# Tau-masked attention with a gated FFN on one core: the last half block as a plain transpose, k and q loaded first, new planner numbers

## The chip, the cores and the metric

The kernel runs on one core of a Trainium2 chip. The metric is the device time of one execution in microseconds, the median of several runs; lower is better.

## What is computed

All tensors are float32 in memory, with batch 8, 8 heads, sequence 576, head width 64, and a hidden width of 1024.

```python
scores = scale * q @ k.T                       # per batch and head, 576 x 576
thresh = scores.max(-1) - tau
scores = where(scores >= thresh, scores, -1e9)
attn   = softmax(scores)                       # divided by sum + 1e-9
x      = (attn @ v), heads side by side        # 8 x 576 x 512
h      = relu(x @ w_in)                        # 512 -> 1024
gate   = sigmoid(conv3(h) along the sequence, one filter of 3 per channel)
out    = (h * gate) @ w_out                    # 1024 -> 512
```

## The kernel before

**Work.** A batch's 576 tokens are cut into tiles of 128 rows: four whole ones and one of 64. Tiles 0 and 1 make one chunk, tiles 2, 3 and 4 another, so there are 16 chunks, and for each chunk four pairs of heads: 64 pairs. A *unit* is one tile of one pair. For a whole tile it takes the two heads one after the other; for the tile of 64 rows both heads share the 128 partitions. Per unit:

- `mm` in `unit` (L442 for the first batch and for the 64-row tiles, on half arrays; L449 else) multiplies q and k into a PSUM buffer `ps_s`, of which there are two.
- `top` (L457, VectorE) takes the row maximum, `exp` (L463, ScalarE) the exponential into `em`, `limit` (L460) the threshold, `mask` (L466, VectorE) zeroes what is under it and sums. After the mask the `ps_s` buffer is free.
- `guard` (L483), a reciprocal (L490) and `even` (L487) give scale and shift, and `norm` (L495) normalises `em`.
- `transposes` turns `em` in blocks of 128 columns on TensorE (L519) into one of two PSUM buffers `ps_t`, and ScalarE copies them out to `eT` (L514). 576 columns are four and a half blocks. For whole tiles the two heads lie side by side, nine blocks; the ninth blocks of all tiles of a pair are collected in one `ps_t` buffer, `group(8, ...)`. In the 64-row tile the last half block of each head goes into the same buffer by `halves` (L534): two ordinary matmuls with half an identity, which put the heads' results on the lower and the upper 64 partitions.
- `attend` (L571) multiplies `eT` with v once per pair, and the result is split in a high and a low part `x`.

After the four pairs of a chunk, `mm1` (L600) computes a 128-channel slice of the hidden layer in three products of high and low parts, followed by ReLU, the three taps (L618, L627), a tanh and the gate. `mm2` (L665) multiplies the gated hidden values with `w_out`, again in three products, for 128 tokens at a time.

**Weights.** They arrive as 64-bit words and `split` turns each into a high and a low float32 part with two operations on ScalarE, two or three on VectorE and one or two on GpSimd. This happens in 16 pieces beside the attention of the first batch. The first three pieces are loaded by ScalarE's queue, all other loads by SyncE's.

**Order.** No order is written by hand. Every operation is entered by `op` with an engine, a cost in ns, a rank (the unit it belongs to, less an `ahead`), and sometimes other engines that may take it. `Plan.run` then plays the program: each engine takes the ready operation of lowest rank, operations may go to another engine when their own has more than `BACKLOG` ns in hand, `LATENCY` is the time from one engine's end to another's start, `SWITCH` the cost of a change of kind on TensorE ("rows" for L442, "cols" for L571, "turn" for L519 and L534, "full" for the rest), and `KEEP` how far in rank TensorE may look to avoid one. `WRATE` sets when weights are due, `MOE` how first-layer and second-layer pieces alternate. The order in which operations were taken is the order of each engine's instructions; on the chip an engine runs them strictly in that order, so a waiting instruction holds all behind it.

Of the kernel before, what the change touches and what calls it, by code (L numbers as in the profile page):

```python
# [20 lines left out]
AHEAD = {'s': 6.0, 't': 3.5, 'a': 3.5, 'prep': 4.0, 'w': 2.0, 'load': 4.25}  # L21

LATENCY = {"pe": 197.0, "act": 145.0, "dve": 130.0, "pool": 115.0, "sp": 2000.0}
HPB = 3
MOE = (2, 1)
BACKLOG = {'pool': 28000.0, 'dve': 500.0, 'act': 9000000000.0}
WRATE = (0.891, 1.015)
# [9 lines left out]
    "rows": {"cols": 190, "turn": 240, "full": 290}, "cols": {"rows": 230, "turn": 260, "full": 310},  # L37
    "turn": {"rows": 95, "cols": 95, "full": 85}, "full": {"rows": 95, "cols": 95, "turn": 5},
}

KEEP = 1.2
# [20 lines left out]
class Plan:  # L62
# [13 lines left out]
    def op(self, engine, ns, fn, w=(), r=(), ahead=0.0, other=None, kind=None):  # L76
# [15 lines left out]
        self.ops.append((((engine, ns), *(other or ())), self.rank - ahead, fn if other is not None else lambda e: fn(), before, bufs, kind))  # L92

    def run(self):
# [28 lines left out]
        while events:  # L123
            t = events[0][0]
            while events and events[0][0] <= t:
# [9 lines left out]
                elif kind == "done":  # L135
                    engine = taken[x]
                    for j in after[x]:
                        waits[j] -= 1
                        for e in came[j]:
                            late = 0.0 if e == engine == "pe" else LATENCY[engine] + (30.0 if e == "pool" != engine else 0.0)  # L140
# [66 lines left out]
def tile_tau_attention_gated_ffn(  # L207
# [54 lines left out]
    op("sp", 100, lambda: nc.sync.dma_start(tau_sb[:], tau.broadcast_to([P, 1])), w=[(tau_sb, 0)], ahead=100.0)  # L262
# [19 lines left out]

    def act(n, psum=False):
        return n * 0.833 + (170 if psum else 200)

    def dve(n, fixed=140):
        return n * 1.1 + fixed

    def pool(n):
        return n * 2.1 + 240  # L290

    def pool1(n):
        return n * 1.69 + 80

    def split(src, n, name, high, low, hr, lr, queue="sp"):
# [37 lines left out]
        op(queue, 450, load, w=[hi, lo], ahead=w + (AHEAD["load"] if queue == "sp" else 90))  # L333
        op("act", act(n), f0, w=[a], r=[hi], ahead=w)
        op("pool", n * 1.69 + 80, f1, w=[a], ahead=w, other=[("dve", 150 + n * 0.65)])
        op("dve", 150 + n * 0.55, f2, w=[a], ahead=w)
        op("dve", 150 + n * 1.1, f3, w=[a], r=[hi], ahead=w)
        op("dve", 150 + n * 1.1, f4, w=[a], r=[lo], ahead=w)
# [43 lines left out]
    def prep_rows(i, b, p, o, w, tag):  # L382
# [4 lines left out]
        op("sp", 450, lambda: nc.sync.dma_start(k[:], kp[b, p]), w=[(k, 0)], ahead=a + 2)  # L387
        op("sp", 450, lambda: nc.sync.dma_start(q[:], qd[b, p, :, :, o:o + w]), w=[(q, 0)], ahead=a + 2)
        op("act", act(2 * w), lambda: nc.scalar.activation(q[:], q[:], AF.Copy, scale=0.125), w=[(q, 0)], ahead=a)
        return k, q  # L390

    def prep_k(b, p, j, ks):
# [3 lines left out]
        op("sp", 820, lambda: nc.sync.dma_start(xk[:, :S], kd[b, p, :, j]), w=[(xk, 0)], ahead=a + 2)  # L396
# [7 lines left out]
    def prep_q(i, b, p, j, q1, q2):  # L404
# [4 lines left out]
        op("sp", 455, lambda: nc.sync.dma_start(xq[:], qd[b, p, :, j, o:o + w]), w=[(xq, 0)], ahead=a + 2)  # L409
# [6 lines left out]
    def load_v(i, b, p):  # L416
        vt = plan.buf(wk, "v", 2, [P, NBLK + 1, D], F32, f"v_{i}")
        op("sp", 820, lambda: nc.sync.dma_start(vt[:], vc[b, p]), w=[(vt, 0)], ahead=AHEAD["prep"])
        return vt

    def unit(u, k, q1, q2, o, n):
# [9 lines left out]
        tiny = [("pool", 290)]  # L431
        for h, js in enumerate(heads):
# [26 lines left out]
            def limit(e, nm=nm, th=th):  # L459
                engines[e].tensor_scalar(few[:rows, th], few[:rows, nm], -1.0, tau_sb[:rows], op0=ALU.mult, op1=ALU.subtract)  # L460
# [4 lines left out]
            def mask(ps=ps, th=th, view=view, total=total):  # L465
# [6 lines left out]
                "pe", 480 if q2 is None else 532, mm, w=[(ps, 0)],  # L472
                r=[(k, 0), (q1, 0)] if q2 is None else [(x, h) for x in (k, q1, q2)], ahead=a, kind="rows" if q2 is None else "full"
# [342 lines left out]
```

## Time and profile before

| | us |
|---|---|
| median of 3 runs (975.6 to 979.25) | 976.28 |
| the profiled execution's own time | 977.8 |
| its span, first to last instruction | 976.0 |
| TensorE busy | 925.7 |
| VectorE busy | 804.6 |
| GpSimd busy | 728.6 |
| ScalarE busy | 694.8 |

In the profile PE is TensorE's matmul, PEld its weight load, DVE is VectorE, ACT ScalarE, POOL GpSimd, SP SyncE; SPq and ACTq are the queues on which those engines issue DMAs. Rows name a source line, the tile written and the tiles read. In a timeline a row is start, duration, engine, line, operation, and, in brackets, how long the engine stood idle before it and what released it.

### The profile page before, as it was taken

To read this page: it belongs to the slowest core of one execution; us is meant where nothing else is said; L and a number is where in the kernel's file an instruction comes from. 1 tells how busy PE (TensorE), PEld (TensorE's weight loads), DVE (VectorE), ACT (ScalarE), POOL (GpSimd) and SP (SyncE) were. 2 spreads that over 40 slices of the span, in tenths; PEclk is the share of its full clock that TensorE was granted. 3 is DMA by queue.
4 is the path that set the end of the run, shared out by engine and by line. 5 is a ranking of instruction groups with operands and counts; after the bars stand their busy time and mean duration, and the time that the engine had idled before them with its cause. 6 is when DMAs were issued, how large, how long until landed. Compare 5 with 4: busy or idle time off the path is not lost.

```text
span 976.0 us, 19384 instructions
## 1 busy us (share of the span) xinstructions
PE 925.7 (95%) x6368; PEld 740.6 (76%) x6368; DVE 804.6 (82%) x1926; ACT 694.8 (71%) x1508; POOL 728.6 (75%) x1175
## 2 busy tenths in 40 slices
PE   3887779999999999999999999999999999999998
PEld 2554558878888878878888788887888878887796
DVE  4889989997988887887897879897897879988443
ACT  4766778777876778767876678777876778776443
POOL 3769898876888678887886769886776877786333
PEclk9999989999999999999999999999999999999999
DMA  6344223233322133213332223223332133311000
GB/s 224 122 146 142 80 85 115 73 91 98 94 93 80 61 104 112 85 53 105 99 106 63 81 84 108 86 74 95 104 99 76 52 102 109 100 50 46 23 22 33
DMA packets 56259, 87.26 MB, mean 89 GB/s; under 512 B 13152, under 2 KB 29536, under 8 KB 56160
## 3 DMA queue, kind: packets, MB, share of 16 engines
q1 hardware_dynamic: 55728, 84.46, 28.5%
q10 hardware_dynamic: 432, 1.57, 0.5%
q8 instruction: 51, 0.84, 0.4%
q14 instruction: 48, 0.39, 0.1%
HBM read 76.57 MB, written 9.44 MB: 88 GB/s over the span
## 4 chain that ended last, share of the span: by engine, by line
PE 74%; DVE 10%; POOL 7%; issue 3%; DMA 2%; ACT 2%; SPq 0%; POOLq 0%; DVEq 0%; ACTq 0%
PE ph L600 17%; PE po L665 17%; PE pa L571 13%; PE ps_t L519 12%; PE ps_s L449 11%; PE ps_s L442 3%; DVE em L466 3%; POOL em L495 3%; DMA q<-in_qd_dram 2%; DVE few L457 2%; POOL gl L280 2%; DVE t L627 1%; DVE t L634 1%; POOL t L618 1%; PE ps_t L534 1%
## 5 line engine op out<-in xcount | busy, mean ns | idle before, releaser
L495 POOL TENSOR_SCALAR em<-em,few 128x576 f32<-128x576 f32 x288 | 263.5, 922 | 42.4 <-DVE few L490 29.3
L466 DVE SCALAR_TENSOR_TENSOR em<-ps_s,few,em 128x576 f32<-128x576 f32 x288 | 230.1, 811 | 36.3 <-ACT em L463 30.2
L457 DVE TENSOR_REDUCE few<-ps_s 128x1 f32<-128x576 f32 x288 | 212.9, 750 | 56.1 <-PE ps_s L449 39.4
L600 PE MATMUL ph<-x,w1h 128*128 128x322 f32 (+1 forms) x1024 | 251.8, 309 | 0.9 <-ACT hp L615 0.6
L463 ACT ACTIVATE em<-ps_s,few 128x576 f32<-128x576 f32 x288 | 209.0, 740 | 42.0 <-DVE few L457 31.5
L514 ACT ACTIVATE eT<-ps_t 128x512 f32<-128x512 f32 (+2 forms) x384 | 193.8, 532 | 48.0 <-PE ps_t L519 44.8
L519 PE MATMUL ps_t<-ident,em 128*128 128x128 f32 x1280 | 191.5, 279 | 12.0 <-POOL em L495 8.1
L627 DVE SCALAR_TENSOR_TENSOR t<-hp,cw,t 128x255 f32<-128x255 f32 (+1 forms) x256 | 176.6, 693 | 29.8 <-POOL t L618 28.1
L519 PEld LDWEIGHTS ps_t<-ident,em 128*128 128x128 f32 x1280 | 148.9, 142 | 52.3 <-POOL em L495 17.4
L600 PEld LDWEIGHTS ph<-x,w1h 128*128 128x128 f32 x1024 | 177.5, 190 | 7.9 <-issue 3.9
L571 PE MATMUL pa<-eT,v 128*64 128x256 f32 (+1 forms) x1280 | 171.5, 415 | 0.0
L449 PE MATMUL ps_s<-ks,q 128*128 128x288 f32 x896 | 159.4, 306 | 7.8 <-DVE em L466 3.2
L600 PE MATMUL ph<-x,w1l 128*128 128x322 f32 (+1 forms) x512 | 152.1, 297 | 0.0
L449 PEld LDWEIGHTS ps_s<-ks,q 128*128 128x128 f32 x896 | 131.2, 189 | 23.3 <-issue 7.4
L571 PEld LDWEIGHTS pa<-eT,v 128*64 128x64 f32 x1280 | 87.1, 138 | 67.3 <-issue 7.5
L280 POOL TENSOR_TENSOR gl<-t,gh 128x321 fp32r<-128x321 f32 (+13 forms) x184 | 119.3, 660 | 12.2 <-ACT gh L644 10.6
L665 PE MATMUL po<-w2h,gh 128*128 128x512 f32 x288 | 118.4, 411 | 0.0
L665 PE MATMUL po<-w2h,gl 128*128 128x512 f32 x288 | 113.7, 395 | 2.2 <-POOL gl L280 2.2
L665 PE MATMUL po<-w2l,gh 128*128 128x512 f32 x288 | 113.3, 393 | 0.0
L618 POOL TENSOR_SCALAR t<-hp,cw 128x321 f32<-128x321 f32 (+1 forms) x128 | 71.9, 562 | 38.2 <-ACT hp L615 31.3
L600 PEld LDWEIGHTS ph<-x,w1l 128*128 128x128 f32 x512 | 97.3, 190 | 0.3
L280 POOL TENSOR_TENSOR ks<-xk,ks 64x576 fp32r<-64x576 f32 x56 | 81.7, 1460 | 16.5 <-ACT ks L398 10.2
(56 smaller groups left out, 1127.6 us busy)
## 6 DMA issues: line engine op xcount, KB each, us to landing
v<-in_vc_dram SPq DMA_DIRECT2D x64, 320.0 KB, 3.0
xk<-in_kd_dram SPq DMA_DIRECT2D x56, 288.0 KB, 2.9
xq<-in_qd_dram SPq DMA_DIRECT2D x112, 128.0 KB, 2.3
k<-in_kp_dram SPq DMA_DIRECT2D x36, 320.0 KB, 3.1
out_dram<-ot SPq DMA_DIRECT2D x36, 256.0 KB, 2.0
stage<-in_w_out_dram SPq DMA_DIRECT2D x8, 512.0 KB, 3.4
stage<-in_w_in_dram SPq DMA_DIRECT2D x5, 512.0 KB, 4.1
q<-in_qd_dram SPq DMA_DIRECT2D x28, 64.0 KB, 3.2
```

The lines of the kernel that those rows point to most:

```text
L280: engines[e].tensor_tensor(dst, x, y, op=ALU.subtract)
L449: nc.tensor.matmul(ps[:, c, :CH], lhsT=q[:, h, o:o + n], rhs=k[:, h, c * CH:(c + 1) * CH], start=(i == 0), stop=(i == 1))
L457: nc.vector.tensor_reduce(few[:rows, nm], ps[:rows, :, :CH], op=ALU.max, axis=mybir.AxisListType.XY, negate=True)
L463: nc.scalar.activation(view(), ps[:rows, :, :CH], AF.Exp, bias=few[:rows, nm])
L466: nc.vector.scalar_tensor_tensor(view(), ps[:rows, :, :CH], few[:rows, th], view(), op0=ALU.is_ge, op1=ALU.mult, accum_out=few[:rows, total])
L495: engines[e].tensor_scalar(sl, sl, few[:rows, 6 + h:7 + h], few[:rows, 8 + h:9 + h], op0=ALU.mult, op1=ALU.add)
L514: "act", act(w, True), lambda dst=dst, src=src: nc.scalar.activation(dst(), src(pt), AF.Copy),
L519: nc.tensor.transpose(out=pt[:, at:at + P], in_=em[:, b * P:(b + 1) * P], identity=ident[:])
L571: nc.tensor.matmul(pa[j * D:(j + 1) * D, :w], lhsT=vt[:, blk + j, :], rhs=eT[:, blk, :w], start=(r == 0), stop=(r == 4))
L600: nc.tensor.matmul(ph[:, :an], lhsT=w1[w][:, cb, fs], rhs=xs[cb][:, h, :an], start=(cb == 0 and i == 0), stop=(cb == NCB - 1 and i == 2))
L627: nc.vector.scalar_tensor_tensor(t[:, :kn], hp[:, k:kn + k], cw[:, 3 * f + k:3 * f + k + 1], t[:, :kn], op0=ALU.mult, op1=ALU.add)
L665: nc.tensor.matmul(po[:], lhsT=x[:, f, at:at + P], rhs=w[:, f, :], start=(f == 0 and i == 0), stop=(f == NFB - 1 and i == 2))
```

## The change

The change has four parts.

1. `halves` is gone. The 64-row tile's columns 448 to 575 are turned as an ordinary block of 128 (`turn` with block number 3.5). Its upper 64 partitions hold the wanted half block of both heads, and two copies of 64x64, instead of one of 128x64, carry them to `eT`, one of them to the other half of the partitions.
2. In `prep_rows` the first k is issued on ScalarE's queue ahead of the weights, the first q at the head of SyncE's. Where q is scaled for a whole tile, that is done in two halves, one for each head.
3. `limit` adds a stored `ntau` = -tau instead of subtracting tau, so that ScalarE can compute it too, and ScalarE is named among the engines for `limit` and `norm`.
4. The numbers of the planner change throughout, and with them the order of every engine. Some of the diff:

```diff
-AHEAD = {'s': 6.0, 't': 3.5, 'a': 3.5, 'prep': 4.0, 'w': 2.0, 'load': 4.25}
+AHEAD = {'s': 6.0, 't': 3.25, 'a': 3.5, 'prep': 4.0, 'w': 2.0, 'load': 4.0}
-LATENCY = {"pe": 197.0, "act": 145.0, "dve": 130.0, "pool": 115.0, "sp": 2000.0}
+LATENCY = {"pe": 210.0, "act": 145.0, "dve": 110.0, "pool": 75.0, "sp": 2000.0}
-MOE = (2, 1)
-BACKLOG = {'pool': 28000.0, 'dve': 500.0, 'act': 9000000000.0}
-WRATE = (0.891, 1.015)
+MOE = (4, 1)
+BACKLOG = {'pool': 27440.0, 'dve': 700.0, 'act': 9000000000.0}
+WRATE = (0.802, 1.117)
-KEEP = 1.2
+KEEP = 3.293
...
+    ntau = const("ntau", [P, 1], F32)
+    op("dve", 70, lambda: nc.vector.tensor_scalar(ntau[:], tau_sb[:], -1.0, None, op0=ALU.mult), w=[(ntau, 0)], r=[(tau_sb, 0)])
...
-        op("sp", 450, lambda: nc.sync.dma_start(k[:], kp[b, p]), w=[(k, 0)], ahead=a + 2)
-        op("sp", 450, lambda: nc.sync.dma_start(q[:], qd[b, p, :, :, o:o + w]), w=[(q, 0)], ahead=a + 2)
-        op("act", act(2 * w), lambda: nc.scalar.activation(q[:], q[:], AF.Copy, scale=0.125), w=[(q, 0)], ahead=a)
+        if i:
+            op("sp", sp(S + D), lambda: nc.sync.dma_start(k[:], kp[b, p]), w=[(k, 0)], ahead=a + 2)
+        else:
+            op("act", 450, lambda: nc.scalar.dma_start(k[:], kp[b, p]), w=[(k, 0)], ahead=210, late=sp(S + D) + LATENCY["sp"])
+        op("sp", sp(2 * w), lambda: nc.sync.dma_start(q[:], qd[b, p, :, :, o:o + w]), w=[(q, 0), (q, 1)], ahead=a + 2 + 100 * (not i))
...
-            op("dve", 748, top, w=[(few, ("nm", h))], r=[(ps, 0)], ahead=a)
-            op("act", 742, exp, w=[(em, h)], r=[(ps, 0), (few, ("nm", h))], ahead=a)
-            op("dve", 200, limit, w=[(few, ("th", h))], r=[(few, ("nm", h)), (tau_sb, 0)], ahead=a, other=tiny)
-            op("dve", 890, mask, w=[(em, h), (few, ("sum", h))], r=[(ps, 0), (few, ("th", h))], ahead=a)
+            op("dve", 668, top, w=[(few, ("nm", h))], r=[(ps, 0)], ahead=a)
+            op("act", 625, exp, w=[(em, h)], r=[(ps, 0), (few, ("nm", h))], ahead=a)
+            op("dve", 125, limit, w=[(few, ("th", h))], r=[(few, ("nm", h)), (ntau, 0)], ahead=a, other=[("pool", 260), ("act", 110)])
+            op("dve", 738, mask, w=[(em, h), (few, ("sum", h))], r=[(ps, 0), (few, ("th", h))], ahead=a)
...
-            op("pool", 905, norm, w=[(em, h)], r=[(few, "inverse"), (few, "shift")], ahead=a, other=[("dve", 490)])
+            op("pool", 807, norm, w=[(em, h)], r=[(few, "inverse"), (few, "shift")], ahead=a, other=[("dve", 400), ("act", 640)])
...
         def odd(pt):
-            for i, x in enumerate(full):
-                turn(pt, i * P, x[0], 8)
-            if n < P:
-                halves(pt, w)
+            for i, x in enumerate(full + small):
+                turn(pt, i * P, x[0], 8 if x[1] == P else 3.5)
```

**The order at the start.** ScalarE's first rows, with what each waits for (DMAHW stands for a DMA's landing), before:

```order
L316 DMA stage_86<-in_w_in_dram 128x512
L267 ACT_TABLE_LOAD
L267 ACTIVATE warm<-warm 128x1 [waits Pool_49]
L316 DMA stage_101<-in_w_in_dram 128x512
L316 DMA stage_105<-in_w_in_dram 128x512 [waits DMAHW1_49]
L319 ACTIVATE stage_c_f<-stage_c 128x24
L319 ACTIVATE stage_f<-stage_86 128x512 [waits DMAHW2_49]
L389 ACTIVATE q_0_91<-q_0_91 128x512 [waits DMAHW4_49]
L339 ACTIVATE cw<-stage_c_f 128x24 [waits DVE_49]
```

and now, where DMAHW0 is k's landing, DMAHW1 q's, DMAHW2 tau's and DMAHW3 that of the convolution's weights `stage_c`:

```order
L400 DMA k_79<-in_kp_dram 128x640
L270 ACT_TABLE_LOAD
L270 ACTIVATE warm<-warm 128x1 [waits Pool_49]
L322 DMA stage_99<-in_w_in_dram 128x512
L322 DMA stage_101<-in_w_in_dram 128x512 [waits DMAHW0_49]
L322 DMA stage_103<-in_w_in_dram 128x512 [waits DMAHW2_49]
L406 ACTIVATE q_0_77<-q_0_77 128x256 [waits DMAHW1_49]
L406 ACTIVATE q_0_77<-q_0_77 128x256
L325 ACTIVATE stage_c_f<-stage_c 128x24 [waits DMAHW3_49]
L348 ACTIVATE cw<-stage_c_f 128x24 [waits DVE_49]
```

k stands at the head, and q's scaling ahead of all work on weights, but behind two weight loads. SyncE's first issues were tau, the convolution's weights, k, q, and the second k and q; they are now q, tau, the convolution's weights, the second k and q. VectorE's first rows are now:

```order
L265 TENSOR_SCALAR ntau<-tau_sb 128x1 [waits DMAHW2_49]
L331 TENSOR_SCALAR stage_c_f<-stage_c_f 128x24 [waits Pool_49]
L334 SCALAR_TENSOR_TENSOR stage_c_f<-stage_c,stage_c_f 128x24 [waits DMAHW3_49,DVE_49]
L337 SCALAR_TENSOR_TENSOR stage_c_f<-stage_c,stage_c_f 128x24 [waits DVE_49]
L474 TENSOR_REDUCE few_127<-ps_s_0_114 128x1 [waits PE_49]
```

The new `ntau` and the three operations on the convolution's weights stand ahead of the first maximum; before, the same three and one on a weight piece did.

**The order at a ninth block.** TensorE in the second batch, before, at the collecting buffer of a pair with a 64-row tile:

```order
L519 MATMUL ps_t_0_3639<-ident,em_3499 128x128 x4
L519 MATMUL ps_t_8_3647<-ident,em_3327 128x128
L519 MATMUL ps_t_8_3647<-ident,em_3442 128x128
L534 MATMUL ps_t_8_3647<-ident,em_3499 64x64 x2
L600 MATMUL ph_6_3655<-x_2061,w1h 128x322
```

and such a buffer in the same part of the program now:

```order
L542 MATMUL ps_t_0_3667<-ident,em_3608 128x128 x4
L542 MATMUL ps_t_8_3677<-ident,em_3359 128x128
L542 MATMUL ps_t_8_3677<-ident,em_3413 128x128
L542 MATMUL ps_t_8_3677<-ident,em_3608 128x128
L618 MATMUL ph_7_3682<-x_1981,w1h 128x322
```

The two half matmuls have become a third transpose.

**The order between score groups.** TensorE in the middle of the run, before; the next group but one reuses a `ps_s` buffer, and six rows of L600 and the other three rows of `ps_s_0_9392` stand between `ps_s_1_9369` and the first row here:

```order
L449 MATMUL ps_s_0_9392<-ks_0_8638,q_52_9269 128x288
L600 MATMUL ph_1_9379<-x_8364,w1h 128x322
L600 MATMUL ph_1_9379<-x_8364,w1l 128x322
L600 MATMUL ph_1_9379<-x_8364,w1h 128x322
L600 MATMUL ph_1_9379<-x_8366,w1h 128x322
L600 MATMUL ph_1_9379<-x_8366,w1l 128x322
L600 MATMUL ph_1_9379<-x_8366,w1h 128x322
L571 MATMUL pa_9410<-eT_9313,v_9127 64x256 x10
L449 MATMUL ps_s_1_9435<-ks_0_8638,q_52_9258 128x288
```

The groups of the same two pairs (q_51 and q_52) now:

```order
L466 MATMUL ps_s_1_9348<-ks_3_9178,q_51_9159 128x288
L589 MATMUL pa_9357<-eT_9245,v_8951 64x256 x10
L542 MATMUL ps_t_0_9384<-ident,em_9157 128x128 x4
L466 MATMUL ps_s_0_9397<-ks_0_8698,q_52_9254 128x288
L466 MATMUL ps_s_0_9397<-ks_0_8698,q_52_9270 128x288
L466 MATMUL ps_s_0_9397<-ks_0_8698,q_52_9254 128x288
L466 MATMUL ps_s_0_9397<-ks_0_8698,q_52_9270 128x288
L466 MATMUL ps_s_1_9406<-ks_0_8698,q_52_9254 128x288
```

Between the end of one group and the next but one there stood twelve matmuls of the hidden layer, a score group and an attention block; now an attention block, four transposes and a score group stand there.

More of the change, by code (lines that the diff above doesn't have):

```diff
@@ L74, in buf, with op @@
         return b
-    def op(self, engine, ns, fn, w=(), r=(), ahead=0.0, other=None, kind=None):
+    def op(self, engine, ns, fn, w=(), r=(), ahead=0.0, other=None, kind=None, late=0.0):
         i = len(self.ops)
@@ L91, in op @@
             x.left += 1
-        self.ops.append((((engine, ns), *(other or ())), self.rank - ahead, fn if other is not None else lambda e: fn(), before, bufs, kind))
+        self.ops.append((((engine, ns), *(other or ())), self.rank - ahead, fn if other is not None else lambda e: fn(), before, bufs, kind, late))
     def run(self):
@@ L518, in turn @@
         def turn(pt, at, em, b):
-            nc.tensor.transpose(out=pt[:, at:at + P], in_=em[:, b * P:(b + 1) * P], identity=ident[:])
+            nc.tensor.transpose(out=pt[:, at:at + P], in_=em[:, int(b * P):int(b * P) + P], identity=ident[:])
         def turns(pt, b0):
```

100 lines of the change are left out of this document (57 added, 43 removed).

## The prediction

> **What bounds the kernel now.** I read the page first: busy shares, the span in forty slices, the chain that ended last.
>
> ```profile
> span 976.0 us, 19384 instructions
> PE 925.7 (95%) x6368; PEld 740.6 (76%) x6368; DVE 804.6 (82%) x1926; ACT 694.8 (71%) x1508; POOL 728.6 (75%) x1175
> PE   3887779999999999999999999999999999999998
> PE 74%; DVE 10%; POOL 7%; issue 3%; DMA 2%; ACT 2%; SPq 0%; POOLq 0%; DVEq 0%; ACTq 0%
> ```
>
> TensorE (PE) is 95% busy, and its row of tenths is short of 9 only in the first seven slices. A view by stretches (span; PE, PEld, DVE, ACT, POOL busy) says where the limits change:
>
> ```profile
> 0.00:150.00 150.00, 111.19 (x684) 71.62 (x684) 123.52 (x282) 98.83 (x190) 112.67 (x158) 0.93 0.43 135
> 190.00:940.00 750.00, 743.91 (x5235) 609.18 (x5234) 627.42 (x1527) 551.05 (x1218) 567.38 (x938) 1.00 0.28 83
> ```
>
> So there are two regimes. From 190 us to 940 PE is busy 744 of 750: what TensorE issues there is the time. In the first 150 us PE misses 39 us, while VectorE (DVE) is busy 123.5 and idle for its first 9.4 (below): that stage, where the weights are split beside the first attention, is near VectorE's limit. PE work saved there buys little; an earlier start does.
>
> PE's two largest waits after 170 us (total, times, longest) are tiny:
>
> ```profile
> PE ps_s L449 <- DVE em L466: 2.1, 4, 0.8
> PE ps_t L519 <- ACT eT L514: 1.1, 1, 1.1
> ```
>
> **The half block.** The line view gives the pieces (count | busy us, mean ns of one):
>
> ```profile
> L519 PE MATMUL ps_t<-ident,em 128*128 128x128 f32 x1280 | 191.5, 279 | 12.0 <-POOL em L495 8.1 <-ACT eT L514 2.9 <-POOL hp L610 0.4
> L534 PE MATMUL ps_t<-ident,em 128*64 128x64 f32 x128 | 10.9, 249 | 0.0
> L514 ACT ACTIVATE eT<-ps_t 128x64 f32<-128x64 f32 x32 | 7.5, 236 | 0.0
> ```
>
> The change takes out the 128 records of L534 (64 instructions, two passes each) and puts 32 plain transposes in. The mean of one includes the pipeline, so the price must come from start to start. Four transposes, six with the halves, and eight, each between the same first-layer matmuls (L600, 322 columns):
>
> ```profile
> 298.51 0.31 PE L600 MATMUL ph<-x,w1h 128*128 128x322 f32 x1
> 298.66 0.60 PE L519 MATMUL ps_t<-ident,em 128*128 128x128 f32 x4
> 299.02 0.39 PE L600 MATMUL ph<-x,w1h 128*128 128x322 f32 x1
> 299.25 0.31 PE L600 MATMUL ph<-x,w1l 128*128 128x322 f32 x1
> ...
> 303.57 0.32 PE L600 MATMUL ph<-x,w1h 128*128 128x322 f32 x1
> 303.72 0.82 PE L519 MATMUL ps_t<-ident,em 128*128 128x128 f32 x6
> 304.47 0.34 PE L534 MATMUL ps_t<-ident,em 128*64 128x64 f32 x4
> 304.73 0.42 PE L600 MATMUL ph<-x,w1h 128*128 128x322 f32 x1
> 304.99 0.31 PE L600 MATMUL ph<-x,w1l 128*128 128x322 f32 x1
> ```
> ```profile
> 272.43 0.31 PE L600 MATMUL ph<-x,w1h 128*128 128x322 f32 x1
> 272.58 1.03 PE L519 MATMUL ps_t<-ident,em 128*128 128x128 f32 x8
> 273.37 0.40 PE L600 MATMUL ph<-x,w1h 128*128 128x322 f32 x1
> 273.60 0.32 PE L600 MATMUL ph<-x,w1l 128*128 128x322 f32 x1
> ```
>
> From the L600 ahead to the second one behind: 0.74 us with four, 1.17 with eight, so 0.108 per transpose; seven would take 0.74 + 3 x 0.108 = 1.06. Six with the halves take 1.42. Each of the 32 groups saves 0.36 us, mostly what changing to 64-column matmuls and back costs. 28 of them lie after 190 us, where PE is the limit: **-10.0 us**. The four in the first stage count nothing; VectorE hides them.
>
> This prices the new transpose at 0.108, and the dearest reading of the rows is the 279 ns of L519. The Trainium skill, "TensorE: Matmul & The Clock Gate", Part 4, gives about 275 ns for a 128x128 transpose in a kernel's context (for bf16); by it 28 x (0.275 - 0.108) = 4.7 us of the gain would go. The rows above speak against it: 279 is one transpose alone, 0.108 the pace in a run.
>
> On ScalarE (ACT) each group's copy of 236 ns becomes two of 64x64, about 0.24 each: 7.5 us more in an engine 73% busy (551 of 750), hidden by that idle quarter. The pair of ps_t buffers is held 0.2 us longer; the wait behind it is the 1.1 us quoted. Nothing is charged; if that cover goes, at most 32 x 0.24 = 7.7 us.
>
> **The order on PE.** Counting the changes of kind in both orders, the halves counted as transposes: 656 before, 640 after, and the blocks that use a split array (L442, L571) are entered 92 times before, 80 after. What an entry and an exit cost:
>
> ```profile
> 517.67 0.31 PE L600 MATMUL ph<-x,w1h 128*128 128x322 f32 x1
> 517.91 0.71 PE L442 MATMUL ps_s<-k,q 64*64 64x288 f32 x8
> 518.56 0.44 PE L519 MATMUL ps_t<-ident,em 128*128 128x128 f32 x2
> ```
>
> Entry: 0.24 against 0.15 from a first-layer matmul to a transpose above, so 0.09. Exit: 0.65 for four pairs of 288 columns, which at L600's pace (0.15 for 322 columns, so 0.134) would be 0.54, so 0.11 at least. I put an entrance with its exit at 0.3, above the 0.20 of these two, since the matmul behind also starts slow (the L600 after the halves takes 0.26 to its successor, not 0.15); 12 fewer make **-3.6 us**. Bounds: 1.1 (entries alone) and 5.
>
> **The waits that the order adds.** The new costs are shorter (748 to 668 for the maximum, 890 to 738 for the mask), so the order packs score groups closer. One chain holds a ps_s buffer: maximum, exp, mask, and the mask's accumulator read:
>
> ```profile
> L466 DVE SCALAR_TENSOR_TENSOR em<-ps_s,few,em 128x576 f32<-128x576 f32 x288 | 230.1, 811 | 36.3 <-ACT em L463 30.2 <-POOL few L460 3.6 <-POOL hp L610 0.4
> L457 DVE TENSOR_REDUCE few<-ps_s 128x1 f32<-128x576 f32 x288 | 212.9, 750 | 56.1 <-PE ps_s L449 39.4 <-PE ps_s L442 14.9 <-POOL t L618 0.4
> L463 ACT ACTIVATE em<-ps_s,few 128x576 f32<-128x576 f32 x288 | 209.0, 740 | 42.0 <-DVE few L457 31.5 <-DVE few L490 7.5 <-POOL em L495 0.6
> ```
>
> 0.75 + 0.74 + 0.81 = 2.30 us, with about 0.1 for each of four handovers (estimate) 2.7. With PE's start-to-start times, the work between the end of a group and the next but one, which reuses its buffer, has a median of 4.8 us before and 3.5 after; under 3.0 us are 5 of 239 before and 38 after. A short one can wait some 0.1 (3.0 less the 2.7, halved): 38 x 0.1 = 4. The path to the transposes through guard, reciprocal and normalisation tightens too; I give it 0.5. That makes **+4.5 us**; bounds 0 (the planner's slack still holds) and +15 (each of the 38 late by 0.4).
>
> **The start.** The first rows of SyncE, ScalarE, PE and VectorE:
>
> ```profile
> 2.10 1.35 SPq L388 DMA_DIRECT2D q<-in_qd_dram  x1
> 8.84 0.22 ACT L319 ACTIVATE stage_c_f<-stage_c 128x24 f32<-128x24 f32 x1 [6.18 <-DMA stage_c<-in_conv_w_dram]
> 9.40 0.18 DVE L325 TENSOR_SCALAR stage_c_f<-stage_c_f 128x24 uint32<-128x24 uint32 x1 [9.40 <-POOL stage_c_f L322]
> 11.16 2.29 PE L442 MATMUL ps_s<-k,q 64*128 64x288 f32 x8 [11.16 <-ACT q L389]
> 12.55 0.76 DVE L457 TENSOR_REDUCE few<-ps_s 128x1 f32<-128x576 f32 x1 [1.78 <-PE ps_s L442]
> ```
>
> q, issued at 2.10 behind a weight and k, is scaled and releases PE at 11.16. Issued first at 0.7 it could do so by about 6, if it lands in the 3 us that such transfers take in the middle of the run (estimate). But three things now stand in front: on ScalarE's queue the scaling of q comes behind two weight DMAs that wait for k's and tau's landing; VectorE begins with ntau, which waits for tau; and the conv weights' three instructions stay ahead of the first maximum, with their DMA still third on SyncE, now behind q. So the first maximum comes about 10 instead of 12.55: **-2.5 us**, passed on whole since VectorE limits this stage. Bounds: 0 (conv weights land at 10.5) and -6 (all by 6.5). The two late weights are wanted only by the hidden layer, behind the first pairs' attention.
>
> **Small operations.** Of the limits ScalarE gets 8 and of the normalisations none: all 288 stay on GpSimd (POOL), so that edit is worth nothing by itself. But the order moves limits (POOL 77 to 47, DVE 211 to 233) and guards and evens (POOL 129 to 74, DVE 191 to 246).
>
> ```profile
> L460 DVE TENSOR_SCALAR few<-few,tau_sb 128x1 f32<-128x1 f32 x211 | 41.2, 207 | 1.4
> L483 DVE TENSOR_SCALAR few<-few 128x2 f32<-128x2 f32 (+1 forms) x83 | 34.8, 419 | 1.1
> L487 DVE TENSOR_SCALAR few<-few 128x2 f32<-128x2 f32 (+1 forms) x108 | 20.7, 191 | 0.0
> ```
>
> 22 x 0.21 + 55 x 0.29 (34.8 + 20.7 over 191) = 20.6 us more on VectorE, which is then busy about 87% of the steady part. Charged nothing: its idle 16% holds them. The split of q's scaling and the weight rates move work within the first stage only and go with the start.
>
> **The sum.** Against the profiled 976.0 (that execution took 977.8; the median of the runs is 976.28, so the sum is put on the median): 976.3 - 10.0 - 3.6 - 2.5 + 4.5 = 964.7, **964.5 us**.
>
> **The rivals.**
> - *The tight order eats the gain.* The mask is late by 0.4 us at each short reuse of ps_s: the +15 of the bound. For it: 38 short distances instead of 5. Against: where this kernel already has 3.0 to 3.6 us, PE's score waits are nearly nil (2.1 us in all). 964.5 + 10.5 = 975, no change.
> - *The first stage shrinks.* PE misses 39 us there; with costs nearer the trace the planner could give back ten, with the start at its bound: 964.5 - 3.5 - 10 = 951. Against: VectorE's work there, 123.5 of 150, is the same.
> - *Slower: VectorE becomes the limit.* The added guards and evens run on VectorE while GpSimd works, and can stand still behind it:
>
> ```profile
> 337.11 1.43 POOL L280 TENSOR_TENSOR ks<-xk,ks 64x576 fp32r<-64x576 f32 x1 [1.30 <-ACT ks L398]
> 337.29 1.27 DVE L483 TENSOR_SCALAR few<-few 128x2 f32<-128x2 f32 x1
> ```
>
> A 128x2 operation took 1.27 us, and ended as GpSimd's did. Each mask and maximum queues behind such a one. If all that VectorE gains shows on PE, it is 964.5 + 20.6 = 985. Against: VectorE would have 13% of the steady part left. It decides where the masks, not PE, set the pace, which in this kernel is so only in the first 150 us. The Trainium skill, "SBUF — State Buffer", section "SBUF: two separate sides", says that GpSimd and a VectorE operation in a two-port mode exclude each other from a shared port pair for a whole instruction; the row above agrees.
> - *The added transposes cost their full 279 ns* (L519's mean): 28 x 0.17 = 4.8 more, 969. Against: the eight in 1.17 us above. The Trainium skill's "TensorE: Matmul & The Clock Gate", Part 4, would have it so.
>
> **Chances.** The forecast 0.56 (956 to 971); tight order 0.17; first stage 0.11; VectorE 0.09; full-price transposes 0.07. A measurement of this kernel tells about 0.5% from no change: 971.4 and 981.2. Faster: 0.54 + 0.11 + 0.06 + 0.03 = 0.74; same: 0.17; slower: 0.09. The range takes in the tight order and the first stage, 950 to 977, and leaves out VectorE's case and the far end of each of the other two.
>
> **What would show it.** Right: no 64-column transposes, L519's group 1312, and seven transposes between L600 in about 1.06 us; PE busy some 12 us less; the first maximum near 10; PE's waits on the mask (2.1 now) at 4 to 8 in the steady part. Wrong: PE waiting on masks or normalisations for over 12 us there; VectorE over 92% busy; the guards' mean on VectorE over 0.5; or a first attention not earlier than 11 us.

## The result: slower by 3.5%

| | before | after |
|---|---|---|
| median, us (4 runs each) | 977.76 | 1011.91 |
| ratio, 95% interval | | 1.0353 [1.0318, 1.0388] |
| span of the profiled execution | 976.0 | 1010.3 |
| TensorE busy from 150 to 940 us, of 790 | 782.4 | 749.5 |

The forecast was 964.5. After the change the page's first lines, PE's slices and the chain that ended last read:

```profile
span 1010.3 us, 19209 instructions
PE 931.1 (92%) x6272; PEld 739.0 (73%) x6272; DVE 811.7 (80%) x2004; ACT 708.3 (70%) x1556; POOL 700.2 (69%) x1090
PE   5887788998999899999999899998999989999998
PE 45%; DVE 28%; POOL 11%; ACT 8%; issue 6%; DMA 1%; SPq 0%; POOLq 0%; ACTq 0%; DVEq 0%
```

PE's share of the chain fell from 74% to 45%, and VectorE's rose from 10% to 28%, while every engine's share of busy time fell. So no other engine became the bound: the engines wait for one another. The stretches (PE, PEld, DVE, ACT, POOL busy) show where:

```profile
0.00:150.00 150.00, 115.75 (x726) 76.04 (x727) 132.50 (x295) 106.58 (x216) 116.76 (x169) 0.95 0.43 138
190.00:940.00 750.00, 714.20 (x4922) 579.85 (x4921) 612.98 (x1557) 546.00 (x1215) 527.36 (x827) 0.99 0.27 82
```

The first stage is no worse. From 190 to 940 PE misses 36 us where it missed 6. Its waits after 170 us (total, times, longest):

```profile
PE ps_t L542 <- DVE x L600: 20.7, 15, 2.9
PE ps_s L466 <- DVE em L486: 11.8, 13, 1.6
PE ps_t L542 <- POOL gl L283: 1.7, 1, 1.7
PE ps_t L542 <- POOL em L519: 1.1, 2, 0.9
```

The wait for masks grew from 2.1 to 11.8. The largest was not there before: transposes wait for `x` L600. That is `low` in `attend`, the second reader of attention's PSUM buffer `pa`. `pa` takes its turns in the same pair of buffers as `ps_t`, so until `low` has run, the next transposes but one can't start. One such place (timeline, PE's rows complete but for weight loads; on ScalarE and VectorE those that `pa` stands behind):

```profile
566.51 2.91 PE L589 MATMUL pa<-eT,v 128*64 128x320 f32 x20
...
568.80 0.65 POOL L636 TENSOR_SCALAR t<-hp,cw 128x255 f32<-128x255 f32 x1
...
569.35 0.72 PE L459 MATMUL ps_s<-k,q 64*64 64x288 f32 x8
...
569.48 1.80 DVE L645 SCALAR_TENSOR_TENSOR t<-hp,cw,t 128x255 f32<-128x255 f32 x2 [0.40 <-POOL t L636]
...
570.00 0.66 PE L542 MATMUL ps_t<-ident,em 128*128 128x128 f32 x4
...
571.31 0.42 ACT L654 ACTIVATE t<-t 128x255 f32<-128x255 f32 x1 [1.78 <-DVE t L645]
...
571.63 0.42 ACT L597 ACTIVATE x<-pa 128x320 fp32r<-128x320 f32 x1
571.75 0.85 DVE L652 SCALAR_TENSOR_TENSOR t<-t,hp 128x255 f32<-128x255 f32 x1 [0.48 <-ACT t L654]
...
572.52 0.47 DVE L645 SCALAR_TENSOR_TENSOR t<-hp,cw,t 128x255 f32<-128x255 f32 x1
...
572.92 0.48 DVE L600 TENSOR_TENSOR x<-pa,x 128x320 fp32r<-128x320 f32 x1
...
573.54 0.63 PE L542 MATMUL ps_t<-ident,em 128*128 128x128 f32 x4 [2.88 <-DVE x L600]
```

Attention's block ended at 569.42 (its last matmul was issued at 568.99). ScalarE could copy `pa` then, but its next instruction is a tanh, which waits 1.78 us for VectorE's taps, and those waited for GpSimd's first tap. The copy starts at 571.63. Then `low` stands on VectorE behind a gate, which waits 0.48 for the tanh, and a tap. It ends at 573.40: 4.0 us after the block, for two copies of 0.9 together. PE issued a score group and one group of transposes and stood 2.88 us. The queues of four engines, each in order, hold one another here.

### The profile page after: what moved, and what is told of

It is laid out like the page before. It is cut to its first block, busy times and chain, and to the rows that moved or that the text cites. A ratio compares the mean times of both kernels' runs of the same rounds, so it can differ in the third digit from the quotient of the medians.

```text
span 1010.3 us, 19209 instructions
## 1 busy us (share of the span) xinstructions
PE 931.1 (92%) x6272; PEld 739.0 (73%) x6272; DVE 811.7 (80%) x2004; ACT 708.3 (70%) x1556; POOL 700.2 (69%) x1090
## 4 chain that ended last, share of the span: by engine, by line
PE 45%; DVE 28%; POOL 11%; ACT 8%; issue 6%; DMA 1%; SPq 0%; POOLq 0%; ACTq 0%; DVEq 0%
PE po L683 14%; PE ps_t L542 9%; DVE em L486 8%; PE ph L618 8%; PE ps_s L466 7%; DVE t L645 7%; PE pa L589 6%; DVE few L474 5%; POOL em L519 5%; ACT em L483 3%; POOL t L636 2%; DVE t L652 2%; ACT eT L537 2%; POOL gl L283 2%; PE ps_s L459 1%
## 5 line engine op out<-in xcount | busy, mean ns | idle before, releaser
L519 POOL TENSOR_SCALAR em<-em,few 128x576 f32<-128x576 f32 x288 | 260.8, 913 | 90.9 <-DVE few L510 78.0
L483 ACT ACTIVATE em<-ps_s,few 128x576 f32<-128x576 f32 x288 | 212.2, 742 | 48.7 <-DVE few L474 45.0
L618 PE MATMUL ph<-x,w1h 128*128 128x322 f32 (+1 forms) x1024 | 245.2, 307 | 0.2 <-ACT hp L633 0.2
L542 PE MATMUL ps_t<-ident,em 128*128 128x128 f32 x1312 | 201.8, 283 | 32.7 <-DVE x L600 23.2
L645 DVE SCALAR_TENSOR_TENSOR t<-hp,cw,t 128x255 f32<-128x255 f32 (+1 forms) x256 | 174.4, 687 | 67.7 <-POOL t L636 61.8
L537 ACT ACTIVATE eT<-ps_t 128x512 f32<-128x512 f32 (+2 forms) x416 | 203.2, 507 | 32.8 <-PE ps_t L542 30.8
L542 PEld LDWEIGHTS ps_t<-ident,em 128*128 128x128 f32 x1312 | 152.4, 144 | 79.6 <-issue 22.3
L466 PE MATMUL ps_s<-ks,q 128*128 128x288 f32 x896 | 165.3, 310 | 14.0 <-DVE em L486 12.5
L683 PE MATMUL po<-w2h,gh 128*128 128x512 f32 x288 | 119.4, 414 | 2.1 <-ACT gh L662 2.0
L654 ACT ACTIVATE t<-t 128x321 f32<-128x321 f32 (+1 forms) x128 | 56.9, 445 | 91.2 <-DVE t L645 87.7
L652 DVE SCALAR_TENSOR_TENSOR t<-t,hp 128x321 f32<-128x321 f32 (+1 forms) x128 | 72.7, 569 | 31.2 <-ACT t L654 30.9
```

The costliest lines, as they stand in the source:

```text
L466: nc.tensor.matmul(ps[:, c, :CH], lhsT=q[:, h, o:o + n], rhs=k[:, h, c * CH:(c + 1) * CH], start=(i == 0), stop=(i == 1))
L483: nc.scalar.activation(view(), ps[:rows, :, :CH], AF.Exp, bias=few[:rows, nm])
L519: engines[e].tensor_scalar(sl, sl, by, to, op0=ALU.mult, op1=ALU.add)
L537: "act", act(w, True), lambda dst=dst, src=src: nc.scalar.activation(dst(), src(pt), AF.Copy),
L542: nc.tensor.transpose(out=pt[:, at:at + P], in_=em[:, int(b * P):int(b * P) + P], identity=ident[:])
L618: nc.tensor.matmul(ph[:, :an], lhsT=w1[w][:, cb, fs], rhs=xs[cb][:, h, :an], start=(cb == 0 and i == 0), stop=(cb == NCB - 1 and i == 2))
```

## The experiments

PE's **priced work** is an estimate: the sum over an order of what each matmul takes from its start to the next start without a wait, which is the median in the trace of before for its kind, width and neighbours. A trace's time between its first and last matmul, less that, is its **wait**; matmuls that ran longer than priced are in it too. By it the change lowered PE's work by 16.4 us, a little more than the forecast 13.6, and the wait rose by 53:

| kernel | ratio to before, 95% | priced work | wait | of it after 150 us |
|---|---|---|---|---|
| before | 1 | 891.1 | 69.7 | 16.5 |
| after | 1.0353 [1.0318, 1.0388] | 874.7 | 122.5 | 71 |
| 1 old numbers | 0.9867 [0.9851, 0.9883] | 876.2 | 76.4 | 22 |
| 4 halves back | 1.0353 [1.0330, 1.0377] | 887.5 | 111.3 | 64 |
| 5 slack 130 | 0.9968 [0.9956, 0.9980] | 874.3 | 86.2 | 34 |
| 7 old numbers, halves | 0.9939 [0.9917, 0.9961] | 891.5 | 66.6 | 18 |
| 8 before, new costs | 1.0442 [1.0416, 1.0468] | 887.5 | 119.4 | 68 |
| 12 old numbers, slack 130 | 0.9785 [0.9769, 0.9802] | 877.3 | 68.4 | 17 |

**Theory**: the new costs and latencies are too near the bare times, so the planner puts each instruction where it can just be served, and every lateness on the chip becomes a wait of PE. For most instructions an old cost held about 40 to 160 ns more, counted on top of the latency. The new costs are the bare pace: maximum, exp and mask are entered at 668, 625 and 738 ns, and in the trace of before the engine's next instruction, where it did not wait, started a median of 668, 625 and 738 ns behind them. **Rival 1**: another number (`KEEP`, `MOE`, switch costs and so on) did it by reordering. **Rival 2**: the changed code, its copies or its loads, did it. Rival 3 is the prediction's own slower case, VectorE stalled by GpSimd; **rival 4** its variant, that cheaper VectorE costs send VectorE the small work.

**1 to 3: which part of the change.** Number 1 puts all planner numbers back (but the costs of SyncE's DMAs) and keeps the code; number 2 costs and latencies alone, such as

```diff
-LATENCY = {"pe": 210.0, "act": 145.0, "dve": 110.0, "pool": 75.0, "sp": 2000.0}
+LATENCY = {"pe": 197.0, "act": 145.0, "dve": 130.0, "pool": 115.0, "sp": 2000.0}
-        return n * 0.833 + (58 if psum else 95)
+        return n * 0.833 + (170 if psum else 200)
-            op("dve", 738, mask, ...
+            op("dve", 890, mask, ...
```

Number 3 puts back the other numbers alone (`AHEAD`, `MOE`, `BACKLOG`, `WRATE`, `SWITCH`, `KEEP`).

> The changed code (plain transposes, first loads, rules for ScalarE) with every planner number put back to its old value: costs, latencies, switch costs, KEEP, MOE, WRATE, BACKLOG, AHEAD. Theory (the new cost numbers leave the order no slack, so that buffers of the transposes, of attention and of the scores come free late): PE's priced work without waits is 876 us in this order, as in the changed kernel (875), and the waits go back to about what they were before (70 us more than that work, 123 after the change), so about 960 to 968. Rival 1 (another number than the costs): the same time here, 960 to 968. Rival 2 (the changed code costs it: two 64x64 copies per group, the first loads in another order): stays at 1000 to 1015.

> The changed kernel with only the costs and the latencies of the instructions put back; switch costs, KEEP, MOE, WRATE, BACKLOG and AHEAD stay new. Theory (no slack in the new costs): 960 to 975, and PE's wait at the transposes on x low (20.7 us after 170 us) falls below 6. Rival 1 (the order of the other numbers): stays at 1000 to 1015. Rival 2 (the changed code): stays at 1000 to 1015.

> The changed kernel with switch costs, KEEP, MOE, WRATE, BACKLOG and AHEAD put back; the costs and latencies stay new. Theory (no slack in the new costs): stays at 1000 to 1018, with PE's waits on x low and on the mask together over 20 us after 170 us. Rival 1 (the order of the other numbers): 960 to 975. Rival 2 (the changed code): stays at 1000 to 1015.

Measured: 966.0, 965.7 and 1023.1 us (ratios 0.9867, 0.9865 [0.9850, 0.9879] and 1.0451 [1.0435, 1.0466]). The costs and latencies carry the whole loss; rivals 1 and 2 fall. Number 3 ended above the theory's 1000 to 1018: the other old numbers lose some 10 us more beside the new costs, and are worth nothing beside the old ones (966.0 against 965.7). PE's waits after 170 us in number 1:

```profile
PE ps_s L466 <- DVE em L486: 3.0, 9, 0.6
PE po L683 <- POOL gl L283: 1.8, 5, 0.6
PE ps_t L542 <- POOL em L519: 1.2, 3, 0.6
PE ps_t L542 <- DVE x L600: 1.1, 3, 0.4
```

The 20.7 us on `x` are 1.1. The same attention block (the 38th of 64) has its copy and `low` here at once:

```profile
546.70 2.91 PE L589 MATMUL pa<-eT,v 128*64 128x320 f32 x20
...
549.66 0.44 ACT L597 ACTIVATE x<-pa 128x320 fp32r<-128x320 f32 x1 [0.21 <-PE pa L589]
...
550.33 0.48 DVE L600 TENSOR_TENSOR x<-pa,x 128x320 fp32r<-128x320 f32 x1
```

From the last matmul's start to the end of `low` it is 1.6 us instead of 4.4. Over all 64 blocks the median is 1.44 before, 2.13 after and 1.73 here; the ninetieth percentile 2.74, 4.02 and 2.62.

**4 and 7: what the plain transpose is worth.** Both put the 64-column matmuls back, number 4 in the changed kernel, number 7 with all old numbers.

```diff
-            for i, x in enumerate(full + small):
-                turn(pt, i * P, x[0], 8 if x[1] == P else 3.5)
+            for i, x in enumerate(full):
+                turn(pt, i * P, x[0], 8)
+            if n < P:
+                halves(pt, w)
```

> The changed kernel with the last half block turned by 64-column matmuls as before the change; all numbers and the rest of the code stay new (the group is planned at the width of six blocks and a half). PE's priced work without waits rises from 875 to 887 us. If the plain transpose is worth on the path what the rows of before said (10 us, 0.36 for each of 28 groups), this runs 8 to 14 us longer than the changed kernel, 1020 to 1026. If PE's waits in this order take up what PE's work gives (the saving turns into wait), it is within 3 us of it, 1009 to 1015. If the two 64x64 copies are what delays the transposes, it is faster than the changed kernel, below 1005.

> All planner numbers old (as in the first experiment, 966.0 us) and in addition the last half block turned by 64-column matmuls again. PE's priced work is 891.5 us against 876.2 there. Theory (the plain transposes save PE time, which shows where nothing else makes PE wait): 976 to 981, about the kernel before. Rival (the saving is hidden in this order as it was in the new one, where putting the halves back cost 2 us): 965 to 969.

Measured: 1014.0 and 973.1. Against the same code without halves that is +2 in the tight order (the ratios are alike, 1.0353 twice) and +7 (0.9939 against 0.9867) in the one with slack. Number 7 is below the 976 to 981 that the theory gave it, so the term is nearer 7 than 10. In the changed order the saving does not show: 12.8 us less work and 11.2 more wait.

**5, 9 and 10: slack alone.** All new costs stay; the latency behind ScalarE and VectorE is raised by 130 (9: by 65; 10: by 260).

```diff
-LATENCY = {"pe": 210.0, "act": 145.0, "dve": 110.0, "pool": 75.0, "sp": 2000.0}
+LATENCY = {"pe": 210.0, "act": 275.0, "dve": 240.0, "pool": 75.0, "sp": 2000.0}
```

> The changed kernel, all its new costs kept, with only the planner's latency behind ScalarE put from 145 to 275 and behind VectorE from 110 to 240 (130 more each, about what the old costs held above the new ones). Theory (the new numbers leave no slack at the handovers): whichever number holds the slack, it is the slack that counts, so 962 to 980, with PE's wait on x low (20.7 us) below 5. Rival 4 (it is the ratio of the costs: cheaper VectorE costs send small operations to VectorE, which then is late): the costs are as after, so the split of the guards is about as after and the time stays above 1000.

> As the slack experiment (new costs; 130 more latency behind ScalarE and VectorE gave 976.1 us against 1011.9), with half of it: 65 more. Theory (slack at the handovers, in proportion): between the two, 985 to 1000. If a threshold decides (the buffers of attention, whose reuses within 1.2 us go from 26 to 6 here and to 0 with 130): 975 to 985. If 976 was a lucky order and not the slack: 1000 or more.

> As the slack experiment with twice as much: 260 more latency behind ScalarE and VectorE, costs still new. Theory (slack): no longer than 976, and towards the 966 of the old costs: 962 to 972. If the other 10 us between 976 and 966 belong to the costs themselves (which engine takes the small operations): 972 to 980. If too much slack spreads the order and empties PE elsewhere: above 980.

Measured: 1011.9 without, 992.2 with 65, 976.1 with 130, 973.1 with 260 (ratios 1.0353, 1.0127 [1.0105, 1.0148], 0.9968, 0.9930 [0.9915, 0.9945]). By the ratios that is 22, 38 and 41 us less than after, of the 48 that the old numbers give. The time falls with the dose and levels off. The last step ended above the theory's 962 to 972, in the range of its second case: some 7 us are left to the costs and the other latencies. But two numbers that touch no cost give back most of the loss. PE's wait on `x` in number 5 was 6.5 us, a little over the 5 expected. Rival 4 falls too. The guards and evens on VectorE in number 5, then in the kernel after:

```profile
L503 DVE TENSOR_SCALAR few<-few 128x2 f32<-128x2 f32 (+1 forms) x121 | 40.2, 332 | 1.5
L507 DVE TENSOR_SCALAR few<-few 128x2 f32<-128x2 f32 (+1 forms) x141 | 27.8, 197 | 0.0
```
```profile
L503 DVE TENSOR_SCALAR few<-few 128x2 f32<-128x2 f32 (+1 forms) x111 | 36.9, 332 | 0.9
L507 DVE TENSOR_SCALAR few<-few 128x2 f32<-128x2 f32 (+1 forms) x135 | 28.2, 209 | 0.0
```

VectorE has more of them than after, at about the same mean, in a kernel that takes 36 us less.

**6, 13, 14, 15 and 16: where the slack was missing.** Each puts some old numbers back in the changed kernel: 6 the cost of the copies `high` and `low` out of `pa` alone, 13 the score chain's, 14 the copies' and the hidden layer's, 15 all costs, 16 the latencies. For number 6:

```diff
-        op("act", act(w, True), high, ...
-        op("dve", dve(w), low, ...
+        op("act", act(w, True) + 112, high, ...
+        op("dve", dve(w) + 75 + w * 0.03, low, ...
```

> The changed kernel with the old cost in the two instructions that free attention's buffer alone: ScalarE's copy x high (112 more) and VectorE's x low (about 80 more), 64 of each. By the priced times the reuses of an attention buffer within 1.2 us go from 26 to 3 of 63. If this buffer is the seat of the loss: PE's wait on x low falls from 20.7 to under 5 us and the time by 15 to 30, to 982 to 997. If the lack of slack is spread over all chains: the wait on x low goes, others take its place, and the time stays above 1000. If x low is late because VectorE is late (rival 4): the wait stays above 10 and the time above 1005.

> The changed kernel with the old costs in the score chain alone (maximum, exp, limit, mask, guard, reciprocal, even, normalisation). If the seat is the reuse of the score buffers, as my prediction's term had it: 970 to 985. If the lack is spread over the chains: 985 to 1002, PE's waits on the mask (11.8 after 170 us) gone and those on x low left. If the seat is the chain of the copies and the hidden layer: 1002 or more.

> The changed kernel with the old costs of the copies and of the hidden layer alone: ScalarE's copies, VectorE's x low and taps, GpSimd's subtractions and first taps. If VectorE's and ScalarE's queues in the hidden layer are the seat (x high and x low stand behind a tanh and a gate that wait for the taps): 966 to 982. If the lack is spread over the chains: 982 to 1000, with PE's wait on x low below 8 and that on the mask left at about 10. If the seat is the score chain: 1000 or more.

> The changed kernel with all old costs and the new latencies. If the costs hold the slack: 964 to 976, near the 965.7 with both put back. If the latencies carry it: 990 or more.

> The changed kernel with the old latencies alone (20 more behind VectorE, 40 more behind GpSimd, 13 less behind PE, the extra 30 instead of 60). At the rate of the half dose (65 more behind ScalarE and VectorE gave 20 us), 20 to 40 more are worth 5 to 10 us: 1000 to 1010. If the latencies carry the loss: below 990.

| put back | us | ratio, 95% | less than after, of the ratio, in us |
|---|---|---|---|
| 6 `high`, `low` | 1001.1 | 1.0225 [1.0198, 1.0252] | 13 |
| 13 score chain | 982.8 | 1.0045 [1.0027, 1.0062] | 30 |
| 14 copies, hidden layer | 981.1 | 1.0028 [1.0015, 1.0040] | 32 |
| 15 all costs | 967.2 | 0.9879 [0.9857, 0.9901] | 46 |
| 16 latencies | 1003.2 | 1.0243 [1.0218, 1.0268] | 11 |

(The last column is the difference of the ratios times 978.) Number 6 ended just above the 1000 that I had named for a lack spread over all chains. It took the named wait from 20.7 to 7.2, yet the one on masks stayed and one on `eT` came: PE's waits after 170 us there,

```profile
PE ps_s L466 <- DVE em L486: 11.7, 14, 1.6
PE ps_t L542 <- DVE x L600: 7.2, 10, 1.4
PE ps_t L542 <- ACT eT L537: 6.5, 5, 1.8
```

and in number 13, where only the score chain's costs are old, most of the wait on `x` goes as well:

```profile
PE ps_s L466 <- DVE em L486: 7.4, 10, 1.2
PE ps_t L542 <- DVE x L600: 3.1, 5, 1.6
```

Either half of the costs gives back two thirds of the loss, and both together 46, not 62. So there is no one seat. I read it so: slack for any chain lets the queues of VectorE and ScalarE run ahead for all of them, since they are shared. Number 13 bears this out in part, since tanh and taps kept their new costs there, and yet ScalarE's tanh waited 51.3 us for taps after 170 us instead of 83.9:

```profile
ACT t L654 <- DVE t L645: 51.3, 49, 2.3
```

The same wait on `x` was cut in two ways. In number 6 attention's buffer comes back as late as after (from the last matmul's start to the end of `low` the ninetieth percentile is 4.07 us, after it was 4.02), but the planner puts its next use farther off. In number 13 short distances remain (16 of 63 under 1.2 us, after it was 26), but the buffer comes back sooner (3.07). Numbers 13 and 14 each ended in the range that I had named for the only seat, which can't hold of both: I had not foreseen that their gains overlap. Number 13 also kept 7.4 us of the wait on masks, which it should have removed.

**8: the costs in the code of before.** The diff is number 2's with its signs turned, on the kernel before, as far as that has the lines.

> The kernel before, its code as it was (halves, load order, limits), with the new costs and latencies of its instructions alone. Theory (the new costs take the slack, whatever the code): 1005 to 1030, with PE waiting on x low and on the mask in the steady part. Rival 2 (the code has its part in the loss): less than 995.

Measured 1022.1, ratio 1.0442: 43 us are lost without any of the changed code. PE's waits there after 170 us:

```profile
PE ps_t L519 <- DVE x L582: 20.4, 27, 2.3
PE ps_s L449 <- DVE em L466: 7.3, 11, 1.1
```

**11: the first loads.** Old numbers, and k, q and tau loaded in the order of before; for k:

```diff
-        if i:
-            op("sp", sp(S + D), lambda: nc.sync.dma_start(k[:], kp[b, p]), w=[(k, 0)], ahead=a + 2)
-        else:
-            op("act", 450, lambda: nc.scalar.dma_start(k[:], kp[b, p]), ...
+        op("sp", sp(S + D), lambda: nc.sync.dma_start(k[:], kp[b, p]), w=[(k, 0)], ahead=a + 2)
```

> All planner numbers old (966.0 us in the first experiment), and the first loads as before the change: k on SyncE's queue and q's load without its lead, so that the first attention starts later. If the early start is passed on whole, as the prediction had it: 2 to 5 us longer than 966.0, 968 to 971. If VectorE's stage behind it absorbs the start: 965 to 967. If the first loads cost something elsewhere (weights that land later): below 965.

Measured 968.8, ratio 0.9887 [0.9872, 0.9902] against number 1's 0.9867: 2 to 3 us, with intervals that touch, so the sign is likely and the size isn't settled. VectorE's first maximum starts at 12.02 there and at 10.19 in number 1.

**12: a version that beats both.** The changed code, the old numbers, and 130 more latency behind ScalarE and VectorE:

```diff
-LATENCY = {"pe": 197.0, "act": 145.0, "dve": 130.0, "pool": 115.0, "sp": 2000.0}
+LATENCY = {"pe": 197.0, "act": 275.0, "dve": 260.0, "pool": 115.0, "sp": 2000.0}
```

> All planner numbers old, and 130 more latency behind ScalarE and VectorE on top: the trial of a version that beats both kernels by more. In the first experiment's order PE still loses some 21 us to waits after 150 us, by the priced times. Theory (slack): some of it goes, 955 to 965. If the old numbers hold enough slack already: 964 to 968. If more of it spreads the first 150 us, where PE waits for VectorE, the time rises: 968 to 980.

Measured **959.0 us**, ratio 0.9785 [0.9769, 0.9802]. Its stretch from 150 to 940 us and PE's largest waits after 170 us:

```profile
150.00:940.00 790.00, 781.62 (x5480) 647.11 (x5479) 657.84 (x1613) 591.79 (x1328) 607.74 (x1002) 1.00 0.28 83
PE ps_t L542 <- POOL em L519: 3.2, 5, 1.2
PE po L683 <- POOL hp L630: 1.4, 2, 0.8
PE ps_s L466 <- DVE em L486: 0.8, 1, 0.8
```

No transposes wait for `x` among them, and masks cost 0.8. This order enters split-array blocks 92 times, as often as before, and is the fastest: here slack was worth more than fewer changes of kind.

## Why the prediction was wrong, point by point

**The half block, -10.0: the pace held, the size came out nearer 7.** After the change, seven transposes between first-layer matmuls:

```profile
356.69 0.28 PE L618 MATMUL ph<-x,w1h 128*128 128x256 f32 x1
356.81 0.93 PE L542 MATMUL ps_t<-ident,em 128*128 128x128 f32 x7
357.49 0.36 PE L618 MATMUL ph<-x,w1h 128*128 128x256 f32 x1
357.69 0.28 PE L618 MATMUL ph<-x,w1l 128*128 128x256 f32 x1
```

That is 1.00 us between 256-column matmuls; between 322-column ones, as in the forecast, the two places in this trace took 1.07 where 1.06 was forecast. The Trainium skill's "TensorE: Matmul & The Clock Gate", Part 4, gives about 275 ns for a 128x128 transpose in a kernel's context (for bf16); an estimate by it for the seven is 1.9 us. The trace does not bear that out. On the path 7 us showed, and only where PE does not wait otherwise (numbers 1 and 7); the rest of the 10 was taken by waits.

**The order on PE, -3.6**: 80 entries, as counted. Against number 1's 88, priced work is 1.5 us less. With the halves put back, the new order has 887.5 us of it (number 4) against 891.1 before, 3.6 less. So the work is about as forecast; no run shows this term alone in the time, and here it drowns in the waits.

**The waits, +4.5 with a bound of +15: this step failed.** The code's own terms sum to -12.5 (half block and start), and number 1, which has the code without the numbers, measured 13 less than before. (That the sums agree so well is partly luck: measured one by one the two are worth 7 and 2 to 3, and some 3 us have no run.) So all of the miss lies in the numbers: after less number 1 is 1.0353 - 0.9867 of 979, 48 us, where the order's and the waits' terms together said +0.9. Two things were wrong in that step. It took each chain alone and at its bare durations: 2.7 us from a group's end to its buffer's return, with the lateness bounded at 0.4, while the chains share VectorE and ScalarE, whose queues are strictly in order; a chain is late by what stands ahead of it, some 3 us in the block above. And it looked only at `ps_s`. Of the other ring it said "The pair of ps_t buffers is held 0.2 us longer; the wait behind it is the 1.1 us quoted. Nothing is charged". Attention's buffer takes its turns in that pair. The same count of distances for it, PE's work from the end of an attention block to the next use but one, gives 1 of 63 under 1.2 us before and 26 after. That was to be had from the order.

What the cover was worth is seen in the wait of tanh for taps. ScalarE's total for it after 170 us, before and after:

```profile
ACT t L636 <- DVE t L627: 13.9, 29, 1.7
```
```profile
ACT t L654 <- DVE t L645: 83.9, 64, 3.4
```

An idle ScalarE was read as cover; in order, an idle engine that waits is a closed door.

**The start, -2.5: right as far as tried.** First maximum at 10.36 (forecast 10); number 11 puts the worth at 2 to 3 us, in the order of the old numbers and with intervals that touch:

```profile
8.98 2.29 PE L459 MATMUL ps_s<-k,q 64*128 64x288 f32 x8 [8.98 <-ACT q L406]
10.36 0.76 DVE L474 TENSOR_REDUCE few<-ps_s 128x1 f32<-128x576 f32 x1
```

**Copies and small operations, nothing: right as far as tried.** Numbers 1 and 5 contain the 64x64 copies, number 5 also more small work on VectorE, and lose nothing visible by them; no run takes them alone.

**The rivals.** The slower end came by none of those listed. VectorE did not become the limit: it was busy 613 of 750 us, 82%, and the guards' mean fell from 419 to 332 ns. The exclusion on a shared port that the Trainium skill names ("SBUF — State Buffer", section "SBUF: two separate sides") did not decide the time: number 1 has the same 334 ns mean. "The tight order eats the gain" had late masks right in kind, but allowed 15 us for it, a third of the loss, and did not have the larger wait, that for attention's buffer. Of the signs of being right, the mask wait (4 to 8 forecast) was 10.5 from 190 to 940 us, and PE's busy time rose from 925.7 to 931.1 instead of falling by 12. Of the signs of being wrong, PE waiting on masks or normalisations for over 12 us was the near one: 10.5 and 1.1 there. The main wait stood under a name that was not on the list.

## What to carry to other kernels

When a planner sets the order for engines that each run in order, a cost that is true to the bare pace was too small here: it leaves no room for lateness, and lateness in one queue is handed on to the others. Before trusting an order that packs tighter, count for every ring of buffers, not only the one that waits now, how much work lies between a release and its reuse, and compare it with the ninetieth percentile of the release in the trace, not with the sum of durations. A short distance is a risk and not yet a loss, as number 13 shows. Slack can be bought with one number, a latency, and its dose can be measured: 65, 130 and 260 ns gave 22, 38 and 41 us here.

## What was not expected of the hardware

In the kernel with the waits the matmuls took longer too. The 1130 transposes after 150 us, in the kernel after and in number 1:

```profile
L542 PE MATMUL ps_t<-ident,em 128*128 128x128 f32 x1130 | 171.0, 281 | 27.7 <-DVE x L600 22.8 <-POOL gl L283 1.7 <-POOL em L519 1.1
```
```profile
L542 PE MATMUL ps_t<-ident,em 128*128 128x128 f32 x1130 | 162.1, 275 | 3.1 <-POOL em L519 1.2 <-DVE x L600 1.1 <-POOL hp L630 0.6
```

PE is busy 8.9 us longer with them, and idle 24.6 more. Over all PE's work from 150 us on (the same two kernels),

```profile
150.00:1030.00 880.00, 815.36 (x5548) 662.92 (x5546) 679.23 (x1710) 601.72 (x1341) 583.44 (x922) 0.99 0.25 76
```
```profile
150.00:1030.00 880.00, 801.52 (x5566) 661.88 (x5564) 668.48 (x1601) 604.38 (x1356) 613.00 (x1022) 1.00 0.26 76
```

busy time is 815.4 against 801.5, and to the ends of the spans (1010.3 and 965.4) 44.9 against 13.9 are idle: 31 of the 45 us between the spans are idle time and 14 are longer matmuls.

The granted clock, 0.99 against 1.00 in these rows, is some 6 of the 14 (estimate). In the kernel after it was halved in four stretches of 3.4 us between 150 us and the last matmuls. Each began within 1.4 us of the end of a wait of PE of 1.9 to 2.9 us on `x`. One of them, after the wait of 2.88 us shown above, with a second-layer matmul in it and the same one behind it:

```profile
574.90:578.30 3.40, 3.40 (x13) 2.81 (x11) 2.48 (x9) 2.50 (x6) 0.82 (x1) 0.50 0.00 0
575.90 0.63 PE L683 MATMUL po<-w2l,gh 128*128 128x512 f32 x1
579.39 0.40 PE L683 MATMUL po<-w2l,gh 128*128 128x512 f32 x1
```

PE was busy for 13.2 of these 13.7 us, at 0.43 us from one second-layer matmul to the next instead of 0.23. Number 1 has no wait of PE over 1.3 us there, and no such stretch. The clock does not follow each wait: one of 2.89 us, at 692.88, has no such stretch behind it. What the other 8 us are, the runs do not show.
